# Moving stores, value loads, weight loads and two second layers in a fused attention and mixture-of-depths kernel

## The chip, the cores and the metric

The kernel runs on one core of a Trainium2 chip. The metric is the device time of one execution in microseconds (us). Three executions of the kernel before took 146.28, 147.19 and 147.28 us; the median, 147.19 us, is what a changed kernel is compared with. The profile is of one further execution, which took 145.79 us and has a span of 144.1 us from first to last instruction. All positions in time below are us from the start of that span.

## The reference

Four batches, eight heads, 768 positions, head dimension 64. Attention sees the first four keys ("sinks") and a window of the last 128 keys. Its output x (768 rows of 512 for each batch) goes to a mixture of depths: the 128 rows of a batch with the highest gate score pass a two-layer network and are added to themselves with a sigmoid weight; all other rows are returned as they are.

```python
scores = scale * np.matmul(q, k.transpose(0, 1, 3, 2))
keep = is_sink | in_window
scores = np.where(keep, scores, -1000000000.0)
a = np.exp(scores - np.max(scores, axis=-1, keepdims=True))
a = a / (np.sum(a, axis=-1, keepdims=True) + 1e-09)
x = np.matmul(a, v)                       # then heads side by side: (4, 768, 512)
for b in range(B):
    s = x[b] @ w_gate
    top_idx = np.argpartition(-s, capacity)[:capacity]        # capacity 128
    ye = np.maximum(x[b, top_idx] @ w1, 0.0) @ w2             # 512 -> 1024 -> 512
    out[b, top_idx] = x[b, top_idx] + sigmoid(s[top_idx])[:, None] * ye
```

## The kernel before, in words

**Units.** Attention is cut into blocks of 128 query rows: six blocks j = 0 to 5 for each batch b. One call of `unit(b, j, gs)` does one block, for the head groups in `gs` (group 0 is heads 0 to 3, group 1 heads 4 to 7). Batch 0 runs its six blocks for group 0 and then again for group 1, because its inputs are still arriving; batches 1 to 3 do both groups in one unit. A unit named (b, j) below is that of group 1 or of both. Within a unit, `scores` multiplies keys by queries and ACT takes the exponential (L315); `pv`, `pv_halves` and `pv_sinks` multiply probabilities with values (L380, L367, L352); `normalize` divides (L387, L390) and gives the block x of the output. The sink part and normalization of a block are done at the start of the next unit, by `close()`.

**Work woven in.** In units 2 to 5 of a batch, `transposes` brings the next batch's keys and queries into the layout that the scores need. In the units of batch b, the selection of batch b-1 runs in steps (`moe_steps`): column sums in unit (b, 1), row numbers and the gather of the chosen rows `xe` in (b, 2), their transposition `xeT` in (b, 4), in (3, 3) for the last batch. The two-layer networks of batches 0 and 1 (`mlp_steps`) run in units of batch 3: each `next` does one layer, the first by L484, the second (`ye`) by L490 followed by a scatter with addition to the output (L496). `layers_mid` and `layers_late` say in which unit; mid comes after the block's value products and after `xeT`, late a little further on. The network of batch 2 and all of batch 3 come in `moe_last`.

**Order.** It is written out by hand: each engine executes its instructions in program order, and so does each queue of transfers. Plain transfers are issued by the SP queue: values (`load_v`), weight sixteenths (`load_w`), stores of x (L397), and for the last batch a second copy of x to `x_last` (L399), from which the last gather reads. Keys and queries from hp 2 of batch 0 on are issued by the Pool queue (L125), since they change type on the way. Pool also converts each weight sixteenth to bf16 (`cast_w`, L242), packs sink keys (L264) and issues gathers and scatters.

**Pace of the loads.** A load gets a gate: it waits until a named instruction is done, the last exponential so far (`exps[-1]`) or the last value product (`late[0]`). `unit` calls `loads(b, j, gs, 0)` after the unit's scores and `loads(b, j, gs, 1)` at its end. The first call issues keys and queries, and values: block j of batch b+1 in unit (b, j). The second issues further keys and queries, the conversions of the sixteenths loaded in the unit before, and then the new sixteenths of `w_loads`. A sixteenth is 128 x 512 fp32; sixteenths 0 to 7 are the first layer's, 8 to 15 the second's. They share four buffers (tags kf and qf, two each), so a fifth load waits for the first conversion. Values have one buffer for each parity of the batch.

**Stores.** In the kernel before, `finish_block` issues the store of x as soon as a block is normalized, in program order ahead of that unit's loads.

## Time and profile before

| what | before |
|---|---|
| median of three executions | 147.19 us |
| span of the profiled execution | 144.1 us |
| TensorE matmul (PE) busy | 124.3 us, 86% of the span |
| TensorE weight load (PEld) busy | 97.7 us, 68% |
| VectorE (DVE) busy | 90.2 us, 63% |
| ScalarE (ACT) busy | 78.7 us, 55% |
| GpSimd (POOL) busy | 53.2 us, 37% |
| bytes moved by transfers | 27.61 MB, mean 192 GB/s |
| granted TensorE clock | 0.99 |

A busy share is time in which the engine worked, over the span; it is an average over stages that differ. The chain of work that ended last starts at the last instruction and goes back, at each step, to whatever released it; where it says "issue", the engine waited for nothing that the profile can name. A line of instructions shows start, duration, engine, source line and what is written from what. A stretch shows how long each engine was busy in it, how many instructions it did, and the mean busy share of the core's 16 DMA engines; since packets overlap, that share can pass 1. Queue q1 carries what SP issues, q0 what Pool issues, and q8 and q14 carry instructions.

### The profile page before, as it was taken

How to read it: one execution, taken by the hardware profiler on the slowest of the kernel's cores; microseconds unless marked ns; L12 is line 12 of the kernel's file. 1: busy time of each engine (PE TensorE's matmuls, PEld its weight loads, DVE VectorE, ACT ScalarE, POOL GpSimd, SP SyncE). 2: the span in 40 equal slices, each digit the busy share in tenths (PEclk: the TensorE clock that was granted, in tenths of full speed). 3: DMA queues.
4: the chain of work that ended last, by engine and by line, in shares of the span. 5: the costliest groups of instructions: out<-in, count | busy, mean ns of one | idle time of the engine just before them, and what ended most of it. 6: DMA issues, size and time to landing. Idle time of an engine off the chain costs nothing.

```text
span 144.1 us, 6776 instructions
## 1 busy us (share of the span) xinstructions
PE 124.3 (86%) x2921; PEld 97.7 (68%) x2921; DVE 90.2 (63%) x294; ACT 78.7 (55%) x168; POOL 53.2 (37%) x111
## 2 busy tenths in 40 slices
PE   6878999999999997879999784969999999999800
PEld 2344887787777986768698674856996885677400
DVE  5644445577969977484998562839992442985020
ACT  3367554875589565175946560749584682343300
POOL 5485143333322354242340752253255400434220
PEclk9999999999999999999999999999999999999995
DMA  4979389699999999999399999959583564580801
GB/s 138 323 130 205 70 133 198 135 194 269 249 289 251 207 246 239 231 292 225 124 190 216 317 216 224 329 151 249 192 298 136 173 84 150 106 253 12 134 16 73
DMA packets 41600, 27.61 MB, mean 192 GB/s; under 512 B 26593, under 2 KB 35169, under 8 KB 41570
## 3 DMA queue, kind: packets, MB, share of 16 engines
q1 hardware_dynamic: 32930, 19.96, 47.5%
q0 software_dynamic: 8640, 7.21, 34.2%
q8 instruction: 23, 0.38, 1.2%
q14 instruction: 7, 0.06, 0.1%
HBM read 24.15 MB, written 8.91 MB: 230 GB/s over the span
## 4 chain that ended last, share of the span: by engine, by line
PE 63%; ACT 11%; issue 10%; DMA 9%; DVE 3%; SPq 1%; POOLq 1%; ACTq 0%
PE xg L380 17%; PE xg L367 11%; ACT pt L315 8%; PE trp L256 8%; PE sc L292 7%; PE xg L352 6%; DMA qf<-in_q_dram 4%; PE sc L309 3%; DMA x_last<-x 3%; PE bc L414 3%; PE hps L484 3%; PE ye L490 2%; DMA out_dram<-gye,idx 2%; DVE cm L420 1%; ACT QT L262 1%
## 5 line engine op out<-in xcount | busy, mean ns | idle before, releaser
L315 ACT ACTIVATE pt<-sc 128x448 f32<-128x448 f32 (+2 forms) x96 | 44.4, 551 | 10.2 <-PE sc L309 9.8
L380 PE MATMUL xg<-vbuf,pt 128*64 128x65 f32 x896 | 34.5, 226 | 1.8 <-issue 1.1
L380 PEld LDWEIGHTS xg<-vbuf,pt 128*64 128x64 f32 x896 | 29.4, 137 | 6.2 <-issue 2.9
L262 ACT COPY QT<-trp 128x768 bf16<-128x768 bf16 x16 | 12.8, 799 | 22.1 <-PE trp L256 22.1
L367 PE MATMUL xg<-vbuf,pt 64*64 64x65 f32 x512 | 21.8, 221 | 1.7 <-issue 1.4
L387 DVE RECIPROCAL rz<-xg 128x4 f32<-128x4 f32 x48 | 8.5, 176 | 22.8 <-PE xg L352 18.3
L292 PE MATMUL sc<-QT,KT 64*64 64x192 bf16 (+3 forms) x384 | 20.5, 252 | 1.9 <-issue 1.4
L390 DVE TENSOR_TENSOR x<-xg,rz 128x256 f32<-128x256 f32 x48 | 20.4, 424 | 1.7
L260 DVE COPY KT<-trp 128x768 bf16<-128x768 bf16 x16 | 15.3, 955 | 9.7 <-PE trp L256 9.7
L367 PEld LDWEIGHTS xg<-vbuf,pt 64*64 64x64 f32 x512 | 19.3, 134 | 2.8 <-issue 1.7
L401 DVE CUSTOM_DVE_ANT_0 junk<-x,wgb 128x512 bf16<-128x512 f32 x24 | 16.9, 704 | 0.8
L292 PEld LDWEIGHTS <-KT 64*64 64x64 bf16 x384 | 11.6, 105 | 8.5 <-issue 4.1
L309 PE MATMUL sc<-msk,ident_b 64*64 64x256 bf16 (+1 forms) x256 | 17.3, 254 | 0.0
L125 POOL DMA_DIRECT2D kb<-in_k_dram x14 | 10.3, 734 | 16.0 <-ACT pt L315 16.0
L242 POOL TENSOR_SCALAR_AFFINE_SELECT w_sb<-wf 128x512 bf16<-128x512 f32 x16 | 10.6, 676 | 13.0 <-DMA wf<-in_moe_w_dram 12.7
L420 DVE SCALAR_TENSOR_TENSOR cm<-sbc,scol,tie 128x128 bf16<-128x128 f32 (+5 forms) x23 | 15.3, 664 | 0.1
L264 POOL TENSOR_SCALAR_AFFINE_SELECT ksk<-KT 64x4 bf16<-64x4 bf16 x32 | 6.3, 196 | 21.9 <-DVE KT L260 14.1
L125 POOL DMA_DIRECT2D qb<-in_q_dram x14 | 10.1, 719 | 10.6 <-ACT pt L315 10.6
L352 PE MATMUL xg<-vsk,psk 64*64 64x260 f32 x128 | 13.4, 400 | 0.0
L256 PE MATMUL trp<-ident_b,kb 128*64 128x128 bf16 x192 | 8.8, 221 | 4.5 <-issue 3.7
L415 ACT COPY sbc<-bc 128x128 f32<-128x128 f32 x23 | 6.4, 276 | 6.3 <-PE bc L414 6.3
L309 PEld LDWEIGHTS <-ident_b 64*64 64x64 bf16 x256 | 9.7, 107 | 0.0
(113 smaller groups left out, 147.6 us busy)
## 6 DMA issues: line engine op xcount, KB each, us to landing
out_dram<-x SPq DMA_DIRECT2D x24, 256.0 KB, 4.5
vbuf<-in_v_dram SPq DMA_DIRECT2D x18, 256.0 KB, 6.9
wf<-in_moe_w_dram SPq DMA_DIRECT2D x16, 256.0 KB, 5.9
kb<-in_k_dram POOLq DMA_DIRECT2D x14, 192.0 KB, 6.1
qb<-in_q_dram POOLq DMA_DIRECT2D x14, 192.0 KB, 5.8
vbuf<-in_v_dram SPq DMA_DIRECT2D x12, 128.0 KB, 3.9
x_last<-x SPq DMA_DIRECT2D x6, 256.0 KB, 4.5
kf<-in_k_dram SPq DMA_DIRECT2D x2, 384.0 KB, 4.0
```

Of the source, the lines that this page charges most:

```text
L125: ins = nc.gpsimd.dma_start(out=ob[:, :, :, :].rearrange(flat), in_=in_)
L256: nc.tensor.transpose(out=trp[es[h], c, :], in_=src[:, h, c, :], identity=ident_b[:])
L260: nc.vector.tensor_copy(out=o, in_=i)
L292: nc.tensor.matmul(out=sc[e][es[kh], hh * w + q0:hh * w + q1], lhsT=st.KT[es[e], hp, k0 + 64 * kh:k0 + 64 * kh + 64], rhs=st.QT[es[e], hp, ...
L309: nc.tensor.matmul(out=sc[e][es[kh], o:o + 2 * w].rearrange("p (h s n) -> p h s n", h=2, n=64)[:, :, sq, :], lhsT=ident_b[es[e], es[e]], r ...
L315: exps.append(nc.scalar.activation(out=pt[:, e, 0:n], in_=sc[e][:, 0:n], func=ACT.Exp, scale=0.125))
L352: ins = nc.tensor.matmul(out=st.xg[j, g][es[m], :, :], lhsT=st.psk[es[g], q0:q0 + 64], rhs=st.vsk[es[g], :, :], **f)
L367: ins = nc.tensor.matmul(out=st.xg[j, g][es[m], hh, :], lhsT=prob(st, j - m, g, hh, es[m], 3 * m), rhs=st.v[es[m], j - m, 4 * g + hh, 0:VS ...
L380: late[0] = nc.tensor.matmul(out=st.xg[j, g][es[m], hh, :], lhsT=prob(st, kc, g, hh, slice(0, 128), s), rhs=st.v[:, kc, 4 * g + hh, 0:VS], ...
L390: nc.vector.tensor_tensor(out=st.x[j][:, 256 * g:256 * g + 256].rearrange("p (h d) -> p h d", h=4), in0=xg[:, :, 0:D], in1=rz[:, :, :].to_ ...
L401: nc.vector.tensor_tensor_reduce(out=junk[:, :], in0=st.x[j][:, :], in1=wgb[:, :], scale=1.0, scalar=0.0, op0=ALU.mult, op1=ALU.add, accum ...
L420: nc.vector.scalar_tensor_tensor(out=cm[:, :], in0=st.sbc[:, 0:n], scalar=st.scol[:, j:j + 1], in1=tie[:, S - n:S], op0=ALU.subtract, op1= ...
```

## The change

Four things change, all of them of order and place; no arithmetic is added or removed.

1. **Stores.** A finished block is noted in a list, and `stores()` issues the list after the loads of the next unit that calls it. It is meant to let loads go ahead of stores that must still wait for x. In the first unit of a batch the gate of the loads becomes the last exponential before the unit, so they may start earlier.
2. **Values.** A table `v_loads` replaces the rule "block j of the next batch in unit j". Loads move nearer to their use and leave units out; the last two blocks of each batch are loaded in the first units of that batch itself.
3. **Weights.** `w_loads` puts the sixteenths near the joins between batches: two in batch 1, four and two in units (2, 0) and (2, 1), four and four in (3, 0) and (3, 1). Before, they were one each in (1, 3) to (2, 3), none in (2, 1), then three, three and four in (2, 4), (2, 5) and (3, 0).
4. **Second layers.** As the second layer's sixteenths now come in later, the second layer of batch 0 moves from (3, 2) to (3, 3), and the first layer of batch 1 goes behind it in (3, 3). The second layer of batch 1 stays in (3, 4).

```diff
     def finish_block(st, j):
-        nc.sync.dma_start(out=out[st.b, j * 128:(j + 1) * 128, :], in_=st.x[j][:, :])
-        if st.b == B - 1:
-            nc.sync.dma_start(out=x_last[j * 128:(j + 1) * 128, :], in_=st.x[j][:, :])
+        to_store.append((st, j))
+        if (st.b, j) == (B - 1, NB - 1):
+            stores()
...
-    layers_mid = {(3, 1): 0, (3, 3): 1}
-    layers_late = {(3, 2): 0, (3, 4): 1}
+    layers_mid = {(3, 1): 0, (3, 3): 0}
+    layers_late = {(3, 3): 1, (3, 4): 1}
...
-    w_loads = {(1, 3): 1, (1, 4): 1, (1, 5): 1, (2, 0): 1, (2, 2): 1, (2, 3): 1, (2, 4): 3, (2, 5): 3, (3, 0): 4}
+    w_loads = {(1, 1): 1, (1, 2): 1, (2, 0): 4, (2, 1): 2, (3, 0): 4, (3, 1): 4}
+
+    v_loads = {(0, 1): [(1, 0)], (0, 2): [(1, 1)], (0, 3): [(1, 2)], (0, 5): [(1, 3)], (1, 0): [(1, 4)],
+               (1, 1): [(1, 5), (2, 0)], (1, 2): [(2, 1)], (1, 3): [(2, 2)], (1, 4): [(2, 3)], (2, 0): [(2, 4)],
+               (2, 1): [(2, 5), (3, 0)], (2, 2): [(3, 1)], (2, 3): [(3, 2)], (2, 5): [(3, 3)],
+               (3, 0): [(3, 4)], (3, 1): [(3, 5)]}
...
-        if nxt and 1 in gs:
-            load_v(nxt, j, slice(0, H), gate=gate)
-            if j == 0:
-                load_sinks(nxt)
+        for s, c in v_loads.get((b, j), ()) if 1 in gs else ():
+            load_v(states[s], c, slice(0, H), gate=gate)
+            if c == 0:
+                load_sinks(states[s])
...
         end = (b, j) == (B - 1, NB - 1)
+        begin = exps[-1]
...
         if j == 0:
...
-            loads(b, j, gs, 0)
+            loads(b, j, gs, 0, begin)
+            stores()
...
         elif end:
+            stores()
...
-            loads(b, j, gs, 0)
+            loads(b, j, gs, 0, exps[-1])
+            stores()
```

## The prediction

> **What bounds the kernel now.** I read the page first, then the chain of waits in order of time, then stretches of the timeline, and last the transfers in short stretches.

> The page shows a TensorE that hardly rests, and a transfer system that is full for half of the run:

> ```profile
> PE 124.3 (86%) x2921; PEld 97.7 (68%) x2921; DVE 90.2 (63%) x294; ACT 78.7 (55%) x168; POOL 53.2 (37%) x111
> DMA  4979389699999999999399999959583564580801
> PE 63%; ACT 11%; issue 10%; DMA 9%; DVE 3%; SPq 1%; POOLq 1%; ACTq 0%
> ```

> Each digit is 3.6 us: DMA stands at 9 from about 29 to 86 us, with one gap at 68 to 72 us, and well lower after 97 us. The chain is mostly PE, but a tenth is "issue". In order of time the large pieces of it are these:

> ```profile
> 56.83 1.39 issue
> 62.74 0.93 issue
> 81.86 1.41 issue
> 87.77 1.92 issue
> 94.49 1.15 issue
> ```

> With 0.35 at 32.71 and 0.19 at 38.09 that is 7.3 us in which PE stood while its inputs were there: each hole lies in the middle of a row of like matmuls (six scores, hole, two scores). Stretches cut at the ends of the holes show what they share:

> ```profile
> 58.20:63.66 5.46, 4.53 (x127) 4.01 (x127) 3.09 (x11) 3.03 (x7) 1.94 (x5) 1.00 1.19 267
> 83.26:89.68 6.42, 4.50 (x127) 3.82 (x127) 3.32 (x10) 2.18 (x6) 2.22 (x5) 1.00 1.14 216
> 89.68:95.63 5.95, 4.79 (x127) 4.21 (x127) 4.33 (x11) 3.34 (x6) 1.62 (x7) 1.00 0.98 294
> 63.66:68.05 4.39, 4.38 (x127) 3.77 (x127) 2.39 (x7) 1.75 (x5) 1.68 (x4) 1.00 1.03 240
> ```

> Exactly 127 matmuls and 127 weight loads lie between holes; the DMA share (last but one) is about 1. The last row is the 127 after the second hole: no hole there, 4.4 us. So holes can come only once in 127 matmuls, and come when transfers are dense. Transfers asked for in half microseconds show queue q8 moving one block in each such span, for instance from 55.5 to 56:

> ```profile
> q8 instruction: 1, 0.02, 11.8%
> ```

> It moves blocks at 55.5, 61.0, 80.5, 86.5 and 93.0 (each the start of a half), and the five holes end at 58.21, 63.67, 83.27, 89.69 and 95.64: 2.2 to 3.2 us later each time. PE waits for its own instructions, which queue with the data. A page of 127 matmuls takes 4.3 to 5.4 us, so the block may move at most some 2 us after the page begins; under a burst it moves 3 to 4 us after, and the hole is the difference, 1 to 2 us.

> [...]

> **The change part by part.**

> *Stores behind loads: 0.* SP stands waiting for x ("SPq L397 <- DVE x L390: 44.3, 15, 6.5"), so loads behind a store come later than they could. But nobody waits for them: values are used six units later, and PE has no wait on a value load. Behind the moved stores stand only other SP transfers; the gather of batch b-1 needs its last store, which still goes out in unit (b, 0), two units ahead. What this brings is position: in (2, 0), the value load leaves at about 68 instead of 72.13 and a key load at about 68 instead of 70.79, into the gap of the DMA row.

> *Values nearer to use: 0 by itself.* The shortest distance is four units, (1, 4) loaded in (1, 0): from about 42 to 57, against 6.9 us to landing in the page's table of issues. It takes two value loads out of each batch and puts two in; batch 0 (29 to 41 us) gives two up for good. I count its two small holes and the 0.2 us wait for a query load at 39 as saved: **-0.5** (0 to -0.7).

> *Weights, batch 1.* Before, sixteenths leave at 55.05, 60.59 and 66.50. After, two leave at about 50 and 54, with the doubled value loads of (1, 1). The hole at 56.83 keeps its crowd: key and query loads at 54.05 and 54.86, a value load at 54.59, a sixteenth just before. The hole at 62.74 loses the sixteenths at 55.05 and 60.59: I take 0.6 of 0.93. The boundary at 52.3 (127 matmuls before 56.7) had its block at 50.0, just in time, and gets a heavier page: +0.2 (0 to 1.5). Sum **-0.4** (-1.2 to +1.2).

> *Weights, batch 2.* Here is the weight of the change. Before, sixteenths leave at 74.20, 77.36 (two issues, stretched to 80.3), 82.35, then three at 87.5 to 90 and three at 96 to 98. After, four leave at about 72, as soon as the stores of (2, 0) are out, and two at about 78, when the conversions free buffers; none from (2, 2) on. By boundary:
> - 94.49: its page held three sixteenths and a value load, and now holds no sixteenth. Hole gone: -1.15.
> - 87.77: its page held one sixteenth, one value load, the gather and a pair of key and query loads. The sixteenth goes, the pair stays: half, -1.0 (0 to -1.9).
> - 81.86: its page gives up one sixteenth and gets two at 78: 0.
> - 77.3 had no hole (block moved at 74.5). The four sixteenths land across it with two value loads and two key and query loads. The page before 94.49 shows what three sixteenths do, 1.15; but two of the value and key loads have left for 68. I take +0.5, ends 0 and 1.6.
> Sum **-1.65** (-4.5 to +0.6).

> On Pool, the conversions of (2, 1) wait for those four landings; behind them stand a query load, sink packing and the gather of batch 1. Before, Pool waited there too, 5.14 us until 79.76, the gather went out at 82.05, and xeT was needed at 90.2: no cost.

> *Second layers and the last eight sixteenths, batch 3.* In (3, 2) PE loses ye, 1.73 us in the chain, and gets it back in (3, 3) behind xeT. Before, PE reached xeT at 114.17, with the gather (issued 109.65) landed by 113.69. Without ye it comes at 112.4. The gather can leave at 108.8, when the row numbers are ready, if the four conversions ahead on Pool, which ended at 109.49, end sooner; their loads now go out in 1.6 us instead of 2.8. Landing takes 4.0 us as here or 5.8, the page's median: 112.9 to 114.7. Then ye needs the last four sixteenths: their loads wait for the first conversions (from about 106.5, one per 0.6 us), land after 3.9 (the quickest of (3, 0)) to 5.9 us (the page's median), and are converted at 113 to 115. So PE stands 0.6 to 2.6 us that it did not stand before; the instruction block at 109.5, which cost 0.23 there, falls into the same time. I take **+1.3**. On SP, the stores of x for (3, 1) queue behind the four waiting loads; only the last gather, at 133, wants x_last: 0. The scatter of batch 0 leaves about 3.5 us later, behind gye; batch 1's came 8.9 us after it, so the order holds: 0. The tail after 124 is untouched.

> **Sum:** -0.5 - 0.4 - 1.65 + 1.3 = -1.25, so 147.19 - 1.25 = 145.94; I say 145.9.

> **Rivals.**
> - *Relief in full.* [...] Then 87.77, 94.49, 62.74 and half of 81.86 vanish (4.7), batch 0's 0.7 too, and batch 3 costs 1.3: -4.1, 143.1. For it: bytes leave exactly the stretch with the largest holes. Against: key and query loads stay, and holes 56.83 and 81.86 stood in their company.
> - *Moved, not removed.* The burst at 72 to 78 makes new holes at 77.3 (1.5) and leaves 81.86 and 87.77, while 94.49 (1.15), batch 0's 0.5 and batch 1's 0.4 go: 1.5 + 1.3 - 2.05 = +0.75, 147.9.
> - *Slower.* PE's idle at (3, 3) is the full 2.6, the burst costs 1.6, the fuller page at 52.3 costs 1.5, and only 94.49, 0.7 in batch 0 and half of 62.74 (0.47) are saved: 5.7 - 2.3 = +3.4 at the worst, +2 if one of the three is mild: 149.2. For it: eight sixteenths, two values and the gather meet in 102 to 114 us, and ye now stands behind two landings.

> **How the numbers follow.** Forecast 0.42, relief 0.21, moved 0.14, slower 0.23. The forecast lies near the edge of 1% (145.72), so half of it counts as faster: 0.21 + 0.21 = 0.42. Within 1%: the other half and the moved case, 0.35. Slower: 0.23. The range reaches to the relief and to the milder slower case, 143.0 to 149.2; what is beyond, bursts that all bite or none, I hold for 2 in 10 at most.

> **What would show it.** In the chain, no issue near 94, a smaller one near 88, a new one near 77, and q8's blocks early in their pages from 84 to 96. In (3, 3), xeT and ye with PE idle before them, and the gather's landing or a w_sb conversion just ahead. SP's wait for x may stay as long as it is. Wrong would be: holes of 1.4 us at 77 and 52 too, or holes that stay with few bytes in flight, so that key and query loads alone make them; or a wait for a value load, which I cost at nothing.

## The result and the profile after

The changed kernel took 154.57, 154.69, 155.53 and 156.31 us, a median of 155.11 us, against 147.24 us for the kernel before in the same series. The ratio is 1.054, 95% interval 1.044 to 1.064: slower by 5%, above the range of the prediction and on the other side of its forecast. The profiled execution has a span of 152.8 us, 8.7 more than before. In the later series single runs of the kernel before took from 144.59 to 151.55 us, and the ratios below are taken against its quickest runs, so a ratio of a few per cent is weak; the medians that stand beside some of them are of all runs. e1, e5 and e6 have no ratio and are told by medians and by their traces.

The page after, in the lines that were read before:

```profile
PE 128.1 (84%) x2921; PEld 99.4 (65%) x2921; DVE 90.4 (59%) x294; ACT 78.9 (52%) x168; POOL 52.6 (34%) x111
PEclk9999999999999996899999999999999689999997
DMA  4859599899999999585889999644888507193611
PE 46%; DMA 26%; issue 7%; DVE 6%; ACT 5%; SPq 4%; POOL 2%; POOLq 1%; ACTq 0%
```

The counts of instructions are the same; PE is busy 3.8 us longer, most of it because its clock drops to half for 3.41 us twice (the 6 and 8 in the row PEclk, which come twice); that makes 3.4 us. Transfers now carry 26% of the chain instead of 9%. The chain in order of time says where (start, duration, what):

```profile
104.64 1.77 SPq L403
...
106.51 2.77 DMA wf<-in_moe_w_dram
...
109.39 0.74 POOL w_sb L242
...
110.14 0.62 POOL w_sb L242
...
110.77 3.60 DMA wf<-in_moe_w_dram
...
114.41 5.57 DMA xe<-out_dram,idx
...
120.03 0.61 PE xeT L480 x4
120.64 3.15 PE ye L500 x8
```

Sixteenths of weights land, Pool converts them, more land, and only then the gather leaves, on whose rows PE waits. (L480 is the line of xeT and L500 that of ye in the changed kernel; ten lines were added above them.) PE's waits for the gather, as total, times and longest:

```profile
PE xeT L480 <- DMA xe<-out_dram,idx: 6.0, 2, 4.7
```

The kernel before has no such wait. To see which stage lost the time, I take the start of the same matmul in each timeline: the first scores of (3, 0), and the row numbers (L454 before) of (3, 2). Until there the two programs on PE are the same.

| kernel | to (3, 0) | to row numbers of (3, 2) | from there to the end |
|---|---|---|---|
| before | 96.2 | 12.0 | 35.9 |
| after | 99.2 | 12.0 | 41.7 |
| e4, layers alone | 98.7 | 12.0 | 38.0 |
| e3, weights and layers | 98.6 | 12.0 | 39.5 |
| e9, cover put back | 98.8 | 12.0 | 36.9 |
| e10, last eight earlier, layers as before | 100.1 | 12.5 | 35.0 |

Of the 8.7 us, 5.8 are in the last column. Profiles scatter there too: in the nine kernels that leave the layers of batch 3 where they were (before, e1, e2, e6 to e8, e10 to e12) it runs from 34.9 to 37.2, so 5.8 is good to about 1 us. The 3.0 us in the first column can't be put to the change from two profiles: e4 has the program of before up to (3, 2), on every engine, and its profile is 2.5 us later there too.

### The profile page after: what moved, and what is told of

Its sections match the earlier page's. It is cut to its first block, busy times and chain, and to the rows that moved or that the text cites. A ratio compares the mean times of both kernels' runs of the same rounds, so it can differ in the third digit from the quotient of the medians.

```text
span 152.8 us, 6776 instructions
## 1 busy us (share of the span) xinstructions
PE 128.1 (84%) x2921; PEld 99.4 (65%) x2921; DVE 90.4 (59%) x294; ACT 78.9 (52%) x168; POOL 52.6 (34%) x111
## 4 chain that ended last, share of the span: by engine, by line
PE 46%; DMA 26%; issue 7%; DVE 6%; ACT 5%; SPq 4%; POOL 2%; POOLq 1%; ACTq 0%
PE xg L380 12%; DMA wf<-in_moe_w_dram 10%; DMA xe<-out_dram,idx 8%; PE xg L367 7%; PE trp L256 6%; PE xg L352 5%; PE sc L292 5%; DMA qf<-in_q_dram 4%; ACT pt L315 4%; PE ye L500 3%; DVE x L390 3%; DMA x_last<-x 2%; PE bc L424 2%; PE sc L309 2%; DMA out_dram<-gye,idx 2%
## 5 line engine op out<-in xcount | busy, mean ns | idle before, releaser
L315 ACT ACTIVATE pt<-sc 128x448 f32<-128x448 f32 (+2 forms) x96 | 44.4, 550 | 12.5 <-PE sc L309 12.3
L380 PE MATMUL xg<-vbuf,pt 128*64 128x65 f32 x896 | 35.1, 228 | 0.7 <-ACT pt L315 0.7
L380 PEld LDWEIGHTS xg<-vbuf,pt 128*64 128x64 f32 x896 | 30.0, 140 | 5.1 <-issue 1.6
L367 PE MATMUL xg<-vbuf,pt 64*64 64x65 f32 x512 | 22.0, 221 | 1.2 <-issue 0.7
L390 DVE TENSOR_TENSOR x<-xg,rz 128x256 f32<-128x256 f32 x48 | 20.4, 424 | 1.6
L367 PEld LDWEIGHTS xg<-vbuf,pt 64*64 64x64 f32 x512 | 19.3, 134 | 2.7 <-issue 1.4
L256 PE MATMUL trp<-ident_b,qb 128*64 128x128 bf16 x192 | 8.5, 226 | 2.5 <-DVE qb L142 1.7
```

The lines of the kernel that those rows point to most:

```text
L256: nc.tensor.transpose(out=trp[es[h], c, :], in_=src[:, h, c, :], identity=ident_b[:])
L315: exps.append(nc.scalar.activation(out=pt[:, e, 0:n], in_=sc[e][:, 0:n], func=ACT.Exp, scale=0.125))
L367: ins = nc.tensor.matmul(out=st.xg[j, g][es[m], hh, :], lhsT=prob(st, j - m, g, hh, es[m], 3 * m), rhs=st.v[es[m], j - m, 4 * g + hh, 0:VS ...
L380: late[0] = nc.tensor.matmul(out=st.xg[j, g][es[m], hh, :], lhsT=prob(st, kc, g, hh, slice(0, 128), s), rhs=st.v[:, kc, 4 * g + hh, 0:VS], ...
L390: nc.vector.tensor_tensor(out=st.x[j][:, 256 * g:256 * g + 256].rearrange("p (h d) -> p h d", h=4), in0=xg[:, :, 0:D], in1=rz[:, :, :].to_ ...
```

## The experiments

**e1 to e4: the parts by themselves.** Theory A at this point: Pool executes in order, and the conversions that now stand ahead of the gather hold it (in the profile after, the row numbers are written by 111.81 us, the last of these conversions ends at 114.24, and the gather leaves at 114.41). Theory B: the change crowds transfers, and the holes in which TensorE waits for instruction blocks get longer wherever it does.

e1 is the kernel before with the stores part alone (two places of that edit):

```diff
-        nc.sync.dma_start(out=out[st.b, j * 128:(j + 1) * 128, :], in_=st.x[j][:, :])
+        to_store.append((st, j))
...
-            loads(b, j, gs, 0)
+            loads(b, j, gs, 0, begin)
+            stores()
```

> The kernel before with the stores part alone (stores behind the next loads, earlier gate in the first unit of a batch). Theory A, Pool's order: what the changed kernel lost comes from conversions that stand ahead of the gathers on Pool, so this part is worth nothing: 146.5 to 148 us. Theory B, crowded transfers: every part that moves transfers into others' way makes holes of 1 to 3 us where TensorE waits for instruction blocks: this part 148.5 to 150 us, with a hole near 54 us.

Measured: 147.1 us (143.52 to 148.54), the kernel before 149.25 in the same series. No loss that can be told, as A has it; the profile has no hole near 54.

e2 replaces only the value loads' rule by the table `v_loads`.

> The kernel before with the new table of value loads alone. Theory A: no conversion moves, so 146.5 to 149 us; the hole of 2.6 us near 54 us may come with it, as unit (1, 1) loads two value blocks. Theory B: two value blocks in one unit are what crowds 48 to 54 us, so that hole comes with the half-speed clock behind it, and the time is 150 to 152 us.

Measured: 148.7 us, ratio 1.019 (0.990 to 1.048). Not separable from no change (the median of the kernel before was 149.25); no hole of 2.6 us near 54, which B wanted. But in (3, 2) PE waits 1.0 us, in two pieces, for conversions of the second layer's last sixteenths, a wait that the kernel before does not have; e6, with the same table, has 1.1 us of it.

e3 has the weights and layers alone:

```diff
-    layers_mid = {(3, 1): 0, (3, 3): 1}
-    layers_late = {(3, 2): 0, (3, 4): 1}
+    layers_mid = {(3, 1): 0, (3, 3): 0}
+    layers_late = {(3, 3): 1, (3, 4): 1}
-    w_loads = {(1, 3): 1, (1, 4): 1, (1, 5): 1, (2, 0): 1, (2, 2): 1, (2, 3): 1, (2, 4): 3, (2, 5): 3, (3, 0): 4}
+    w_loads = {(1, 1): 1, (1, 2): 1, (2, 0): 4, (2, 1): 2, (3, 0): 4, (3, 1): 4}
```

> The kernel before with the weight table and the second layers of the changed kernel; stores and values stay. Theory A: this carries most of the loss: in (3, 3) TensorE waits 3 us or more for the gather and loses 1 to 1.5 us more to a lower clock behind the wait, 151 to 154 us. Theory B: it carries a third at most, 148 to 150 us, as the transfers of batch 3 are thin.

Measured: 155.24 us (151.82 to 157.13), ratio 1.068 (1.028 to 1.109); by medians of all runs 1.040, and every run is above every run of the kernel before in the series (144.59 to 150.80). These two parts carry most of the loss. B, which allowed them a third, falls. The profile is of the quickest run, 151.82, and has A's wait only in part:

```profile
118.58 0.40 PE L470 MATMUL xeT<-ident_b,xe 128*128 128x128 bf16 x4 [2.57 <-DMA xe<-out_dram,idx]
118.81 1.89 PE L490 MATMUL ye<-w_sb,hT 128*128 128x512 bf16 x8
```

The wait is 2.57 us, not 3, there is a hole of 1.39 us at 114.25 ahead of it, and ye runs at full clock, so the lower clock is not in every execution.

e4 has the first four of those diff lines, and the weights of before.

> The kernel before with the second layers moved and nothing else; all weights come as early as in the kernel before. Theory A: the gather leaves as early as before (about 109.7 us) and TensorE, which no longer has the second layer to do in the meantime, stands 1 to 2 us at xeT: 147.5 to 149.5 us. Theory B: no transfer is moved, so no loss: 146.5 to 147.5 us.

Measured: 150.5 us, ratio 1.036 (1.021 to 1.052), above A's range of 147.5 to 149.5; but the kernel before had a median of 149.25 in this series, so the times alone do not decide between A and B. The trace does. No transfer was moved, and yet PE waits for the gather, which it did not before:

```profile
117.28 0.40 PE L470 MATMUL xeT<-ident_b,xe 128*128 128x128 bf16 x4 [1.78 <-DMA xe<-out_dram,idx]
```

The bracket is PE's idle time before the row and what ended it. So a part of the loss is neither Pool's order nor crowd: the second layer had been covering the gather.

**e5: the late conversions left out.** The changed kernel, with this edit and one line that fills the second layer's weights with zeros at the start; the second layer then multiplies by zeros, so the network's contribution is missing from the output.

```diff
             for i in w_casts:
-                cast_w(i)
+                if i < 8:
+                    cast_w(i)
```

> The changed kernel with the conversions of the second layer's eight sixteenths left out (their loads stay; the second layer multiplies with zeros set once at the start, so the network's part of the output is missing). Theory A, Pool's order: the gather in (3, 2) leaves as soon as the row numbers are there, some 3 us sooner than in the changed kernel; the wait at xeT falls from 4.7 to 1.5 to 2.5 us and the half-speed clock behind it goes: 3 to 5 us faster than the changed kernel, about 150 to 152 us. Rival, crowding: the gather's landing is what is slow, and without conversions the loads stay as dense, so the wait keeps 4 us or more and the time 154 us or more.

Measured: 153.02 us (149.81 to 157.57); the profile is of the slowest run, so it is read for order and not for time. The first half of A held: the gather leaves 0.8 us after the row numbers are written (116.81; row numbers 115.90 to 116.06) instead of 2.6 in the changed kernel. The second did not:

```profile
122.82 0.49 PE L481 MATMUL xeT<-ident_b,xe 128*128 128x128 bf16 x4 [3.46 <-DMA xe<-out_dram,idx]
```

The wait falls from 4.74 to 3.46, not to 2, and half speed follows it (122.99 to 126.40), since the gather itself takes 6.0 us to the first xeT, while the last sixteenths and two blocks' stores move (1.40 MB by SP's queue from 116.8 to 122.9). Pool's order alone was too simple; the account below has three terms.

**e9: cover put back.** The changed kernel, with the first layer of batch 1 at the place in (3, 2) that the second layer of batch 0 had left. It gets a buffer of its own for its result, as the second layer of batch 0 comes later.

```diff
-    layers_late = {(3, 3): 1, (3, 4): 1}
+    layers_late = {(3, 2): 1, (3, 4): 1}
...
-        hT = mp.tile([128, 8, 128], BF16, name="hT", tag="hT")
+        hT = mp.tile([128, 8, 128], BF16, name="hT", tag="xr" if st.b == 1 else "hT")
```

> The changed kernel with one layer put back as cover: the first layer of batch 1 runs late in (3, 2), where the second layer of batch 0 stood, and the second layer of batch 0 stays in (3, 3). Conversions, loads and gathers keep their order. If the loss at xeT is that TensorE comes there with nothing left to do, 1.8 us of the wait go, and the half-speed clock behind it[...]: 2 to 3.5 us faster than the changed kernel, 151.5 to 153 us. Rival, that the conversions of the last four sixteenths hold ye anyway: under 1 us gained.

Measured: 151.48 us, ratio 1.033 (1.020 to 1.047), by medians of all runs 1.021; at the near edge of what was expected. The wait at xeT in batch 3 falls by 3.5 us:

```profile
117.56 0.40 PE L480 MATMUL xeT<-ident_b,xe 128*128 128x128 bf16 x4 [1.22 <-DMA xe<-out_dram,idx]
117.80 1.89 PE L500 MATMUL ye<-w_sb,hT 128*128 128x512 bf16 x8
```

and ye runs at full clock. That is more than the 1.8 us of cover: in this profile the gather also left sooner, 0.4 us after the row numbers, as the first four conversions ended at 111.6. So e9 does not measure the cover by itself.

**e10: the batch 3 parts undone.** The changed kernel with the last eight sixteenths a unit earlier and the layers of before (the two lines of the layers are left out here).

```diff
-    w_loads = {(1, 1): 1, (1, 2): 1, (2, 0): 4, (2, 1): 2, (3, 0): 4, (3, 1): 4}
+    w_loads = {(1, 1): 1, (1, 2): 1, (2, 0): 4, (2, 1): 2, (2, 5): 4, (3, 0): 4}
```

> The changed kernel with the last eight sixteenths a unit earlier, four in (2, 5) and four in (3, 0), and the layers as in the kernel before. Stores, values and the burst in (2, 0) and (2, 1) stay. Theory A, as it stands now (batch 3 makes the loss): from the row numbers of (3, 2) to the end 36 to 37.5 us instead of 41.7; the time 147 to 150.5 us. Rival, that the burst of (2, 0) costs as much: over 151.

Measured: 149.73 us, ratio 1.016 (0.999 to 1.032), by medians of all runs 1.009. The last column of the table falls from 41.7 to 35.0, as low as in kernels that never had the change there, and the larger part of the 5.4% is gone. What is left may be nothing or 3%.

**e7 and e8: are the holes what I took them for?** e7 is the kernel before with 40 small matmuls more in the warm-up.

```diff
     keep_warm(10)
+    shift = ps.tile([128, 512], FP32, name="shift", tag="ps")
+    for _ in range(40):
+        nc.tensor.matmul(out=shift[:, 0:64], lhsT=warm[:, 0:128], rhs=warm[:, 0:64], start=True, stop=True)
```

> The kernel before with 40 small matmuls more in the warm-up, while TensorE waits for the first keys. If TensorE's holes are waits for blocks of its own instructions, every hole comes 40 matmuls earlier in the program and still a multiple of 127 matmuls from the others (at counts that leave 95 when divided by 127). Rival, that the holes are data waits which the profile can't name: they stay with the same instructions. The time stays within 1.5% of the kernel before either way.

Measured: 148.75 us, ratio 1.006 (1.002 to 1.010). In the kernel before, one hole stood after 5 of 12 key transposes of unit (2, 3):

```profile
81.53 0.33 PE L256 MATMUL trp<-ident_b,kb 128*64 128x128 bf16 x5
83.27 0.38 PE L256 MATMUL trp<-ident_b,kb 128*64 128x128 bf16 x7 [1.41 <-issue]
```

In e7 it stands in the same unit before the last 3 of 32 matmuls of L367, with 32 of L380 between them and the transposes:

```profile
81.86 1.09 PE L367 MATMUL xg<-vbuf,pt 64*64 64x65 f32 x29
84.42 0.33 PE L367 MATMUL xg<-vbuf,pt 64*64 64x65 f32 x3 [1.48 <-issue]
```

3 + 32 + 5 = 40: the hole moved by just the matmuls put in. It belongs to the instruction stream, not to any datum. The others agree: counted over the trace, the matmuls ahead of each of the five largest holes called "issue" leave 95 when divided by 127 in the kernel before, and 94 in e7, whose trace lacks four matmul records.

e8 is the kernel before with the value loads of batches 1 to 3 left out (`load_v(nxt, j, ...)` deleted, and `vbuf[1]` set once to 0.5).

> The kernel before with the value loads of batches 1 to 3 left out (attention there uses the values of batch 0, or a constant), which takes out 18 transfers of 256 KB in 256-byte packets. If holes grow with the transfers in flight, those in batches 0 to 2 sum to 3 us or less instead of 7, and the time falls by 3 to 5 us, to about 143. Rival, that keys, queries and weights make them alone: 5 us or more of holes stay.

Measured: 140.57 us, ratio 0.949 (0.934 to 0.964). Over the same matmuls, from 24 us to (3, 0), PE's pauses above 0.5 us, counted as start-to-start time above 0.2, sum to 7.2 us in the kernel before and to 1.8 in e8. All of them stand at ends of 127. That is 5.4 of the 5.9 us by which the two profiles differ (144.1 and 138.2). So the holes are instruction blocks that wait behind transfers, and are worth about what the prediction said.

**e6, e11, e12: what of the change is worth keeping.** e6 has the stores and values of the changed kernel and the rest of before. e11 is e6 with the sixteenths spread:

```diff
-    w_loads = {(1, 3): 1, (1, 4): 1, (1, 5): 1, (2, 0): 1, (2, 2): 1, (2, 3): 1, (2, 4): 3, (2, 5): 3, (3, 0): 4}
+    w_loads = {(1, 3): 1, (1, 4): 1, (1, 5): 1, (2, 0): 1, (2, 1): 1, (2, 2): 1, (2, 3): 1, (2, 4): 1, (2, 5): 4, (3, 0): 4}
```

e12 has the same line, with stores as changed and values as before.

> Stores and values of the changed kernel, weights and layers of the one before: the changed kernel without the parts that put conversions ahead of the gathers. Theory A: no loss against the kernel before, ratio 0.985 to 1.01. Rival, that the two parts crowd 48 to 54 us and 100 to 115 us by themselves: a ratio of 1.02 or more.

> Stores and values of the changed kernel, layers of the kernel before, and the sixteenths spread: one each in units (1, 3) to (2, 4) and four each in (2, 5) and (3, 0), so that no burst meets key and query loads. If holes follow the crowd, the one near 94 us goes and the others stay: 1 to 2 us under the kernel before. Rival: no difference that can be measured.

> The same spread of sixteenths with the stores of the changed kernel and values as in the kernel before. If the late value loads of (3, 0) and (3, 1) hold up the last conversions, this is up to 1 us faster than the one with moved values; else the two are alike, 1 to 2 us under the kernel before.

Measured: e6 149.23 us, the kernel before 148.16 in its series: no loss that can be told. e11 147.47 us, ratio 0.992 (0.986 to 0.997), by medians of all runs 0.994: faster than the changed kernel, and within 1% of the kernel before. The hole near 94 that was to go is still there, 0.88 us at 97.10 in e11 and 1.70 us at 97.58 in e12. e12 149.26 us, ratio 1.017 (1.009 to 1.026), by medians of all runs 1.006: the expectation that it would match or beat e11 failed. With this spread the moved values are worth 2.5% by the ratios and 1.2% by the medians of e11 and e12; by which hole was not tried.

## Why the prediction was wrong

**What bounds the kernel: right.** The holes are instruction blocks behind transfers (with 40 matmuls more in e7 one moved by just 40; with the value loads out in e8 they fall from 7.2 to 1.8 us).

**Stores 0, values about 0: not contradicted** by e1 and e2; e12 against e11 suggests that the value table can matter with other weights beside it, and so do the waits for conversions in e2 and e6. The saving in batch 0 did not come: where I counted two holes of 0.35 and 0.19 us as gone, the profile after has 0.47, 0.47 and 0.40 us of "issue" at 33.61, 39.11 and 49.46.

**Holes of batch 1: the places wrong.** I left 56.83 as it was and gave 52.3 another 0.2. In the profile after, the two later holes are gone and all of it stands at the earlier boundary, 2.60 us (in e10, which has the same loads there, 2.33):

```profile
56.97 0.39 PE L292 MATMUL sc<-QT,KT 64*64 64x192 bf16 x8 [2.60 <-issue]
```

That is beyond the upper end of my term (1.5), and the half speed behind it adds some 1.7 us (3.41 us at half). How a block's delay depends on the transfers in flight is not shown: in the kernel before, q8's block at 101.86 us moved 0.79 us after its page began and that at 109.83 us 3.89 us after, with a mean DMA share of 0.57 and 0.71 in the 2 us ahead of them.

**Holes of batch 2: about right.** The hole of 94.49 is gone, that of 81.86 stays (1.10), none came near 77, and where that of 87.77 stood, 0.26 us is left and a wait of 0.75 us for a query load follows. But the sentence "On Pool ... no cost" failed. The gather of batch 1 left at 87.86, 5.6 us after its row numbers (82.15 to 82.29), behind the last of these:

```profile
80.41 0.65 POOL L242 TENSOR_SCALAR_AFFINE_SELECT w_sb<-wf 128x512 bf16<-128x512 f32 x1 [2.13 <-DMA wf<-in_moe_w_dram]
81.69 0.61 POOL L242 TENSOR_SCALAR_AFFINE_SELECT w_sb<-wf 128x512 bf16<-128x512 f32 x1 [0.63 <-DMA wf<-in_moe_w_dram]
83.01 0.61 POOL L242 TENSOR_SCALAR_AFFINE_SELECT w_sb<-wf 128x512 bf16<-128x512 f32 x1 [0.71 <-DMA wf<-in_moe_w_dram]
85.84 0.61 POOL L242 TENSOR_SCALAR_AFFINE_SELECT w_sb<-wf 128x512 bf16<-128x512 f32 x1 [2.22 <-DMA wf<-in_moe_w_dram]
...
87.86 1.01 POOL L474 DMA_INDIRECT xe<-out_dram,idx  x1 [0.27 <-POOL ksk L264]
```

I had taken the slack from a gather at 82.05, and compared it with a queue that had one conversion in it, not four that land one after the other. PE waited 1.3 us for those rows (6.0 in all less 4.7), which ate the better part of the gain.

Together I put -2.55 us for all that lies ahead of batch 3. No such gain was seen: e10, which keeps these parts and only brings the last eight sixteenths forward, measured 0.999 to 1.032, where a gain of 2.55 us would be 0.983.

**Second layers and the last sixteenths: the step that failed.** I put +1.3 (0.6 to 2.6); the stage lost 5.8. By its terms:

- *PE comes earlier to xeT, 1.7 us: right.* Before, it came 5.3 us after the row numbers were written (114.10 against 108.81); after, 3.5 (115.29, where PE's last matmul ended, against 111.81): 1.8 earlier. The lines are the row numbers, PE's coming and the gather before, and the row numbers after:

```profile
108.65 0.16 DVE L457 TENSOR_SCALAR idx<-se 128x1 uint32<-128x1 f32 x1 [0.66 <-PE se L454]
109.65 1.00 POOL L464 DMA_INDIRECT xe<-out_dram,idx  x1 [0.15 <-issue]
114.10 0.40 PE L470 MATMUL xeT<-ident_b,xe 128*128 128x128 bf16 x4
...
111.65 0.16 DVE L467 TENSOR_SCALAR idx<-se 128x1 uint32<-128x1 f32 x1 [0.61 <-PE se L464]
```

- *The gather leaves sooner: wrong way round.* I expected it at the row numbers, since the four loads ahead would go out in 1.6 us. They do go out quickly, but only at 106.51, behind a store to x_last that took SP 1.77 us to issue; then they land with a value load beside them, which (3, 0) and (3, 1) did not have before. The conversions end at 114.24, 2.4 us after the row numbers:

```profile
109.39 1.35 POOL L242 TENSOR_SCALAR_AFFINE_SELECT w_sb<-wf 128x512 bf16<-128x512 f32 x2 [9.82 <-DMA wf<-in_moe_w_dram]
113.01 1.23 POOL L242 TENSOR_SCALAR_AFFINE_SELECT w_sb<-wf 128x512 bf16<-128x512 f32 x2 [2.26 <-DMA wf<-in_moe_w_dram]
114.41 1.25 POOL L474 DMA_INDIRECT xe<-out_dram,idx  x1 [0.17 <-DMA wf<-in_moe_w_dram]
```

  Before, the gather left 0.84 us after the row numbers; now 2.60: 1.8 later.
- *Landing 4.0 to 5.8: the upper end, from a start that was misread.* The 4.04 us of the prediction ends with the scatter at 113.69, which the profile has waiting for ACT. The table of transfers gives that gather 3.2 us, and after the change 5.6: 2.4 longer.

```profile
xe<-out_dram,idx POOLq DMA_INDIRECT x1, 3.2
...
xe<-out_dram,idx POOLq DMA_INDIRECT x1, 5.6
```

  In the first case SP's queue moved 0.19 MB between the gather's start and 113.7, in the second 1.43 MB until PE had the rows. Much of that is stores: SP issued those of two blocks, four of 256 KB, from 114.65 to 117.88, behind the last four loads, which had to wait for buffers. I had put that queueing at nothing. That it slowed the gather is argued from these traces, and no run took the stores away.

  1.8 + 1.8 + 2.4, less the 1.25 us by which the gather was early before (109.65 + 3.2 against 114.10), is 4.75: the wait of 4.74.
- *The clock: not in the sum at all.* Stretches with PE busy, and the granted clock third from the end:

```profile
58.54:61.95 3.41, 3.41 (x61) 3.01 (x61) 0.96 (x1) 0.46 (x2) 0.76 (x2) 0.50 0.97 193
...
120.00:123.40 3.40, 3.37 (x11) 1.47 (x12) 0.00 (x0) 0.58 (x1) 0.00 (x0) 0.50 0.16 60
```

  Behind the wait, and behind the hole of 2.60 us in batch 1, PE ran 3.4 us at half speed. Here that made ye 3.15 us in the chain instead of 1.73: 1.4 us. The wait and this are 6.2, near the 5.8 of the stage. It is one execution of each kernel; e3's, with the same weights and layers, has a wait of 2.57 us, full clock, and 3.6 us more than before in the stage.

The rival "slower" had the right place, ye and xeT behind two landings, but at +2 it was as short as the forecast: it too left out the clock, and took the gather's landing for the last link where it was the last of three.

## What to carry to other kernels

Before moving work, write down what each in-order queue holds ahead of the instruction that others wait for, with its landing: a conversion that waits for a load holds the gather behind it (here by 1.8 us in batch 3 and about 5 in batch 1), though Pool is busy only 34% of the span. Ask of a matmul that is moved what it covered where it stood, and put something else there (e9). And count what the clock may do behind a wait on TensorE: after those of 2.60 and 4.74 us in the changed kernel it was 0.50 for 3.41 us, up to 1.7 us lost each time, after one of 2.57 us in e3 it stayed at 1.00; whether it falls is not in the length of the wait alone.

## What the runs showed of the hardware

| run | hole or wait, us | beat | PE busy in it, us | clock in the next beat |
|---|---|---|---|---|
| after | 2.60 | 55.12 to 58.54 | 1.57 | 0.50 |
| after | 4.74 | 116.56 to 119.98 | 0.00 | 0.50 |
| e1 | 1.92 | 87.99 to 91.41 | 1.50 | 0.50 |
| before | 1.92 | 86.49 to 89.90 | 1.49 | 1.00 |
| e3 | 2.57 | 113.96 to 117.38, then to 120.79 | 1.76, 2.21 | 1.00, 1.00 |

  Behind the hole of e1, 13 transposes took 0.87 us, where 11 ahead of it had taken 0.33; ye behind the wait of e3 took 1.73 us in the chain, the time of the kernel before. The beats given for e1 and e3 agree with their mean clocks (0.979 and 0.971) to about 0.15 us. The wait of e3 is divided between two beats and brought no drop. The edge is not sharp (1.50 and 1.49), and busy time is not all that counts: e6 drops near 14.7 us, where 32 matmuls of L380 took 1.93 us (1.08 in e1), although its chain has PE at work for at least 2.4 of the 3.41 us before.
- Waits for TensorE's instruction blocks took some 5% of this kernel (7.2 of 144.1 us): with the value loads out, e8 is 5.1% faster though PE is busy 124.3 us in both. In the kernel before q8 moved 23 blocks, 0.38 MB, each at most one page of 127 matmuls ahead of its use, and at the five large holes the transfer began 2.2 to 3.0 us before PE went on.
- The same program, up to (3, 0), took 96.2 us in one profile and 98.7 in another (before and e4), with holes at the same ends of 127 but of other lengths; differences of that size between two single profiles say nothing.
